# Stores of H and of the rows of x2 issued from ACT's queue instead of SyncE's

## The chip, the cores and the metric

The kernel runs on one core of a Trainium2 chip. The metric is the device time of one execution in microseconds (us). Five engines work side by side, each through its own list of instructions in a fixed order: TensorE (PE, with its weight loads as PEld), VectorE (DVE), ScalarE (ACT), GpSimd (POOL) and SyncE (SP), which computes nothing and issues transfers (DMAs). ACT and POOL can issue transfers too. An instruction that has to wait for a semaphore holds up what stands behind it on its own engine.

## The reference, cut to what matters

```python
scores = (q @ k.T) / sqrt(64); keep = (pos < 4) | ((0 <= rel) & (rel < 128))
x  = softmax(where(keep, scores, -1e9)) @ v       # 4 batches, 8 heads, 768 tokens -> 3072 x 512
H  = max(x @ w1, x @ w2, x @ w3)                  # 3072 x 768
x2 = H @ w_out                                    # 3072 x 512
# routing: tokens go to 8 experts by their logits x2 @ w_gate, 384 tokens to each expert
out[mask_e] = relu(x2[mask_e] @ u1[e]) @ u2[e]
```

## The kernel before, in words

The 3072 tokens are worked on as 8 groups of 384. Numbers are split into a high and a low part (h and l), and a product takes three matmuls: high by high, low by high and high by low.

- **Attention** (class Attn) works on one pair of heads at a time. SP loads kn, qn, vn and vns for it; these tiles have one buffer each. ACT and DVE split them (kh, kz, qs, vsp), PE makes scores, ACT and DVE make the softmax in a tile T, and PE transposes it and multiplies by v.
- **The first mixture** (Moe1.group) makes H for a group: for each of six blocks f, three times 12 matmuls into a PSUM tile mm (two buffers), taken over by ACT (i=0, L274) or DVE (i=1 and 2, L275) into hm (two buffers); ACT then makes hh (L279) and DVE hl (L280). Group 0 stores each hm to DRAM (sp), since w_out isn't there yet; group 5 stores all its hh and hl (sp0h, sp0l to sp5h, sp5l). Both are L282.
- **x2** (Moe1.x2) makes three row tiles of 128 tokens for a group: twice 18 matmuls (L296) into mm, which ACT copies (L298) into the two halves of xo. ACT copies the gate logits out of xo into LG (L306), and L307 stores the 512 columns of xo to x2d in DRAM. The tile xo has one buffer: the next row tile's first L298 can't write until the store before it has landed. This form of x2 runs five times: group 1, then group 0 (its H loaded back from sp by `reload`, L312), then groups 2, 3 and 4. That makes 15 stores. The last three groups use other tiles (xq, three buffers), and their stores were on ACT's queue already.
- **Routing and the second mixture** (Route, Moe2) follow from about 606 us on. They read x2d by indirect loads, and stream the experts' weights through SP.

All of the first part stands in one block whose order, on each engine, is set by a scheduler from priorities and modelled times: code marked `high_priority` is moved forward, attention of group g+1 is spread between the blocks of group g. So a DMA that is moved to another queue can move other instructions too. Each DMA waits on semaphores that the order's rows name: `DMAHW1` is the count of transfers that land on it, and `Activation` or `DVE` a count of instructions that these engines finished.

Of the kernel before, what the change touches and what calls it, by code (L numbers as in the profile page):

```python
# [22 lines left out]
def f32(ap): return ap.bitcast(FT)  # L23
# [179 lines left out]
class Moe1:  # L203
# [49 lines left out]
    def group(s,xs,spill=None,pair=False,pool=None,mid=None,between=None):  # L253

        nc=s.nc; main=s.main
        X=[]
        for p in range(4):
            h=main.tile([128,384],FR,name=f"xh{p}",bufs=1); l=main.tile([128,384],FR,name=f"xl{p}",bufs=1)
            with s.tc.high_priority():
                nc.scalar.activation(h,xs[p],AF.Copy)  # L260
                nc.vector.tensor_tensor(l,xs[p],f32(h),op=OP.subtract)  # L261
            X.append((h,l))
        H=[]
        for f in range(6):
            if between is not None: between(f)
            m=main.tile([128,384],FT,name="hm",bufs=2)
            for i in range(3):
                ps=s.mm.tile([128,512],FT,name="mm")
                n=0
                for p in range(4):  # L270
                    for a,b in ((0,0),(0,1),(1,0)):
                        nc.tensor.matmul(ps[:,:384],s.W[i][a][:,p,f*128:(f+1)*128],X[p][b],start=(n==0),stop=(n==11)); n+=1  # L272
                with s.tc.high_priority():
                    if i==0: nc.scalar.activation(m,ps[:,:384],AF.Copy)  # L274
                    else: nc.vector.tensor_tensor(m,ps[:,:384],m,op=OP.max)  # L275
                if mid is not None and (f,i)==s.at: mid()
            h,l=((pool or main).tile([128,384],FR,name=f"h{x}{f}",bufs=1) for x in "hl")
            with s.tc.high_priority():
                nc.scalar.activation(h,m,AF.Copy)  # L279
                nc.vector.tensor_tensor(l,m,f32(h),op=OP.subtract)  # L280
            if spill is not None:
                for d,x in (zip(spill[f],(h,l)) if pair else ((spill[f],m),)): nc.sync.dma_start(d,f32(x))  # L282
            H.append((h,l))
        return H
    def x2(s,H,t0,LG,x2d,n=260,pool=None,keep=None):

        nc=s.nc; main=s.main
        for t in range(3):
            o=pool.tile([128,512],FT,name="xq",bufs=3) if pool else main.tile([128,520],FT,name="xo",bufs=1)
            for u in range(2):  # L290
                c=slice(0,260) if n==260 else slice(4-4*u,260-4*u)
                ps=s.mm.tile([128,512],FT,name="mm")
                k=0
                for f in range(6):
                    for a,b in ((0,0),(0,1),(1,0)):
                        nc.tensor.matmul(ps[:,:n],H[f][a][:,t*128:(t+1)*128],s.WO[b][:,f,u,c],start=(k==0),stop=(k==17)); k+=1  # L296
                with s.tc.high_priority():
                    nc.scalar.activation(o[:,u*n:(u+1)*n],ps[:,0:n],AF.Copy)  # L298
                    if keep is not None:
                        for d in (2*u,2*u+1):  # L300
                            h,l=keep(t,d); c=ps[:,(d-2*u)*128:(d-2*u)*128+128]
                            nc.scalar.activation(h,c,AF.Copy)
                            nc.vector.tensor_tensor(l,c,f32(h),op=OP.subtract)
            if n==260:
                o,e=s.row(o,0)
                nc.scalar.activation(LG[:,t0+t,:].rearrange("p (u e) -> p u e",u=2),e,AF.Copy)  # L306
            (nc.scalar if pool else nc.sync).dma_start(x2d[(t0+t)*128:(t0+t+1)*128,:],o)  # L307
    def reload(s,spill):
        nc=s.nc; H=[]
        for f in range(6):  # L310
            m=s.main.tile([128,384],FT,name="hm",bufs=2)
            nc.sync.dma_start(m,spill[f])  # L312
            h=s.main.tile([128,384],FR,name=f"hh{f}",bufs=1); l=s.main.tile([128,384],FR,name=f"hl{f}",bufs=1)
            nc.scalar.activation(h,m,AF.Copy)  # L314
            nc.vector.tensor_tensor(l,m,f32(h),op=OP.subtract)
            H.append((h,l))
        return H
# [455 lines left out]
```

## Time and profile before

| | us |
|---|---|
| median of 3 runs (1009.89 to 1012.05) | 1010.73 |
| the profiled execution | 1006.23 |
| its span in the trace | 1004.5 |
| PE busy in the span | 943.2 |
| DVE busy | 715.4 |
| ACT busy | 534.6 |
| POOL busy | 344.9 |

The span runs from the first instruction to the last. An engine's busy time is the time in which at least one of its computing instructions ran; issuing a DMA doesn't count as busy, but it does occupy the engine's place in its own order. PE's busy time is modelled at the end of each matmul, so small gaps hide in it. [...]

### The profile page before, as it was taken

How to read it: one execution, taken by the hardware profiler on the slowest of the kernel's cores; microseconds unless marked ns; L12 is line 12 of the kernel's file. 1: busy time of each engine (PE TensorE's matmuls, PEld its weight loads, DVE VectorE, ACT ScalarE, POOL GpSimd, SP SyncE). 2: the span in 40 equal slices, each digit the busy share in tenths (PEclk: the TensorE clock that was granted, in tenths of full speed). 3: DMA queues.
4: the chain of work that ended last, by engine and by line, in shares of the span. 5: the costliest groups of instructions: out<-in, count | busy, mean ns of one | idle time of the engine just before them, and what ended most of it. 6: DMA issues, size and time to landing. Idle time of an engine off the chain costs nothing.

```text
span 1004.5 us, 18503 instructions
## 1 busy us (share of the span) xinstructions
PE 943.2 (94%) x6594; PEld 860.1 (86%) x6594; DVE 715.4 (71%) x1740; ACT 534.6 (53%) x1431; POOL 344.9 (34%) x307
## 2 busy tenths in 40 slices
PE   4879899989999999999999999989899999999996
PEld 3558799979999989999999998878788788888895
DVE  7989887785977898787754435887888888843320
ACT  5667664896868787688643211323434333454431
POOL 4677555045344535345533000101202111233331
PEclk9999899989999999999999999998999999999999
DMA  7444412231112112112210002623525443553430
GB/s 214 149 140 138 133 62 65 65 99 60 53 37 79 42 44 77 36 46 79 79 44 2 1 1 85 213 87 106 167 65 169 126 146 118 168 189 114 149 105 32
DMA packets 50541, 95.04 MB, mean 95 GB/s; under 512 B 6704, under 2 KB 20784, under 8 KB 50448
## 3 DMA queue, kind: packets, MB, share of 16 engines
q1 hardware_dynamic: 45312, 79.04, 25.4%
q0 software_dynamic: 3840, 12.45, 3.6%
q10 hardware_dynamic: 1296, 2.36, 0.6%
q8 instruction: 52, 0.85, 0.4%
q14 instruction: 41, 0.34, 0.1%
HBM read 77.84 MB, written 16.12 MB: 94 GB/s over the span
## 4 chain that ended last, share of the span: by engine, by line
PE 70%; DVE 11%; DMA 6%; ACT 5%; issue 5%; POOL 1%; SPq 0%; POOLq 0%; DVEq 0%; ACTq 0%
PE mm L272 27%; PE acc L594 11%; PE mm L601 11%; PE mm L296 5%; PE po L181 3%; DMA sa<-in_u_dram 3%; PE rc L399 2%; DMA st<-in_words_dram 2%; PE pp L25 2%; DVE qs L97 2%; PE pt L25 1%; PE po L172 1%; PE ps L126 1%; DVE cA L223 1%; PE ps L127 1%
## 5 line engine op out<-in xcount | busy, mean ns | idle before, releaser
L177 POOL TENSOR_TENSOR L<-A_w,H 128x768 fp32r<-128x768 f32 x46 | 87.4, 1900 | 141.0 <-ACT H L176 133.7
L556 POOL DMA_INDIRECT xg<-x2d,idx x24 | 26.1, 1088 | 192.0 <-PE mm L601 70.3
L275 DVE TENSOR_TENSOR hm<-mm,hm 128x384 f32<-128x384 f32 x96 | 53.2, 554 | 53.8 <-PE mm L272 51.9
L544 ACT ACTIVATE wah<-sa 128x512 fp32r<-128x512 f32 x64 | 40.5, 632 | 94.1 <-PE mm L601 65.4
L544 ACT ACTIVATE wbh<-sb 128x512 fp32r<-128x512 f32 x64 | 40.3, 630 | 73.7 <-PE acc L594 63.1
L594 PE MATMUL acc<-wbh,hh 128*128 128x512 f32 x192 | 78.3, 408 | 0.0
L594 PE MATMUL acc<-wbh,hl 128*128 128x512 f32 x192 | 78.2, 407 | 0.0
L594 PE MATMUL acc<-wbl,hh 128*128 128x512 f32 x192 | 77.7, 405 | 0.0
L296 PE MATMUL mm<-woh,hh 128*128 128x260 f32 (+1 forms) x252 | 73.7, 294 | 1.8 <-ACT hh L314 1.7
L296 PE MATMUL mm<-woh,hl 128*128 128x260 f32 (+1 forms) x252 | 72.2, 292 | 1.6 <-DVE hl L280 1.1
L296 PE MATMUL mm<-wol,hh 128*128 128x260 f32 (+1 forms) x252 | 72.2, 288 | 0.0
L272 PE MATMUL mm<-xh,w1h 128*128 128x384 f32 x192 | 66.8, 348 | 1.6 <-DVE hm L275 0.8
L545 DVE TENSOR_TENSOR wbl<-sb,wbh 128x512 fp32r<-128x512 f32 x64 | 44.1, 689 | 33.8 <-ACT wbh L544 33.7
L272 PE MATMUL mm<-xh,w0h 128*128 128x384 f32 x192 | 67.1, 349 | 0.5 <-DVE hm L275 0.5
L272 PE MATMUL mm<-xh,w2h 128*128 128x384 f32 x192 | 66.6, 347 | 0.8 <-ACT wgt L249 0.4
L272 PE MATMUL mm<-xl,w0h 128*128 128x384 f32 x192 | 65.3, 340 | 1.3 <-DVE xl L261 1.3
L272 PE MATMUL mm<-xh,w1l 128*128 128x384 f32 x192 | 65.7, 342 | 0.0
L272 PE MATMUL mm<-xl,w1h 128*128 128x384 f32 x192 | 65.6, 342 | 0.0
L272 PE MATMUL mm<-xl,w2h 128*128 128x384 f32 x192 | 65.0, 339 | 0.0
L272 PE MATMUL mm<-xh,w0l 128*128 128x384 f32 x192 | 65.0, 338 | 0.0
L272 PE MATMUL mm<-xh,w2l 128*128 128x384 f32 x192 | 64.9, 338 | 0.0
L605 DVE SCALAR_TENSOR_TENSOR hl<-mm,hh 128x384 fp32r<-128x384 f32 x64 | 35.3, 553 | 41.3 <-ACT hh L604 41.0
(315 smaller groups left out, 3090.7 us busy)
## 6 DMA issues: line engine op xcount, KB each, us to landing
sa<-in_u_dram SPq DMA_DIRECT2D x64, 256.0 KB
sb<-in_u_dram SPq DMA_DIRECT2D x64, 256.0 KB
st<-in_words_dram SPq DMA_DIRECT2D x24, 512.0 KB
qn<-in_q_dram SPq DMA_DIRECT2D x24, 192.0 KB
x2d<-xo SPq DMA_DIRECT2D x15, 256.0 KB
kn<-in_k_dram SPq DMA_DIRECT2D x12, 264.0 KB
vn<-in_v_dram SPq DMA_DIRECT2D x12, 256.0 KB
kn<-in_k_dram SPq DMA_DIRECT2D x12, 198.0 KB
```

The source lines that it names most:

```text
L25: nc.tensor.transpose(out,x,f32(ident))
L177: nc.gpsimd.tensor_tensor(L,Af,f32(H),op=OP.subtract)
L181: nc.tensor.matmul(po[:,q:q+n],u['VS'][:,blk,128*h:128*h+128],part[:,c:c+n],start=(part is H and j==0),stop=False,skip_group_check=True)
L272: nc.tensor.matmul(ps[:,:384],s.W[i][a][:,p,f*128:(f+1)*128],X[p][b],start=(n==0),stop=(n==11)); n+=1
L275: else: nc.vector.tensor_tensor(m,ps[:,:384],m,op=OP.max)
L296: nc.tensor.matmul(ps[:,:n],H[f][a][:,t*128:(t+1)*128],s.WO[b][:,f,u,c],start=(k==0),stop=(k==17)); k+=1
L544: nc.scalar.activation(h,src,AF.Copy)
L545: (nc.gpsimd if s.n>=6 and nm=="wa" else nc.vector).tensor_tensor(l,src,f32(h),op=OP.subtract)
L556: nc.gpsimd.indirect_dma_start(out=g,out_offset=None,in_=s.x2d[0:first or 3072],in_offset=bass.IndirectOffsetOnAxis(ap=idx[:,t:t+1],axis=0 ...
L594: nc.tensor.matmul(acc[t],H[f][a][:,t*128:(t+1)*128],W[f][1][b],start=(f==0 and n==0),stop=(f==F-1 and n==2)); n+=1
L601: nc.tensor.matmul(ps[:,:384],W[f][0][a][:,k,:],X[k][b],start=(n==0),stop=(n==11)); n+=1
L605: nc.vector.scalar_tensor_tensor(l,ps[:,:384],0.0,f32(h),op0=OP.max,op1=OP.subtract)
```

## The change

The stores of L282 and L307 are issued by ACT instead of SP. Nothing else in the source differs.

```diff
             if spill is not None:
-                for d,x in (zip(spill[f],(h,l)) if pair else ((spill[f],m),)): nc.sync.dma_start(d,f32(x))
+                for d,x in (zip(spill[f],(h,l)) if pair else ((spill[f],m),)): nc.scalar.dma_start(d,f32(x))
...
             if n==260:
                 o,e=s.row(o,0)
                 nc.scalar.activation(LG[:,t0+t,:].rearrange("p (u e) -> p u e",u=2),e,AF.Copy)
-            (nc.scalar if pool else nc.sync).dma_start(x2d[(t0+t)*128:(t0+t+1)*128,:],o)
+            nc.scalar.dma_start(x2d[(t0+t)*128:(t0+t+1)*128,:],o)
```

33 stores change queue: 6 of sp (group 0), 12 of sp0h to sp5l (group 5) and 15 of x2d. On PE the order is the same for the first 913 rows (up to the end of x2 of groups 1 and 0); behind that attention and first mixture are interleaved otherwise, up to group 6, and the rest is the same again.

ACT, first row tile of x2 in group 1. Before, from the copy of the logits (L306) on to the next row tile's L298:

```order
L96 ACTIVATE qs_2866<-qn 64x384
L306 ACTIVATE LG<-xo 128x8 [waits Activation_49]
L145 ACTIVATE l<-l 128x6 [waits Activation_49]
L134 ACTIVATE T_w<-ps 128x132 [waits PE_49,Pool_49]
L298 ACTIVATE xo<-mm 128x260 [waits DMAHW1_49,Activation_49]
L298 ACTIVATE xo<-mm 128x260
```

The same place in the changed kernel:

```order
L96 ACTIVATE qs_2866<-qn 64x384
L306 ACTIVATE LG<-xo 128x8 [waits Activation_49]
L307 DMA x2d<-xo 128x512 [waits DMAHW1_49]
L145 ACTIVATE l<-l 128x6 [waits Activation_49]
L134 ACTIVATE T_w<-ps 128x132 [waits PE_49,Pool_49]
L298 ACTIVATE xo<-mm 128x260 [waits DMAHW1_49,Activation_49]
L298 ACTIVATE xo<-mm 128x260
```

The store now stands behind L306 on ACT, two short instructions ahead of the L298 that waits for it to land.

SP at the same x2, as a difference (kn and qn are loads of attention, hm the reload of group 0's H):

```order
 L77 DMA qn<-in_q_dram 128x384
 L312 DMA hm<-sp_1038 128x384
-L307 DMA x2d<-xo 128x512
-L75 DMA kn<-in_k_dram 128x528
-L307 DMA x2d<-xo 128x512
+L75 DMA kn<-in_k_dram 128x528
 L77 DMA qn<-in_q_dram 128x384
 L312 DMA hm<-sp_1039 128x384
-L307 DMA x2d<-xo 128x512
 L312 DMA hm<-sp_1040 128x384
```

The loads keep their order and lose the three stores between them; before, the stores did not stand behind L306 but followed the second L298.

ACT, the first block of group 5, whose hh and hl are stored. Before:

```order
L279 ACTIVATE hh_5382<-hm 128x384 [waits DVE_49]
L274 ACTIVATE hm<-mm 128x384 [waits PE_49]
L108 ACTIVATE vsp<-vn 128x4x2x64 [waits DMAHW4_49,PE_49]
L183 ACTIVATE x_5679<-po 64x384 [waits PE_49]
L142 ACTIVATE m<-m 128x6 [waits DVE_49]
```

And in the changed kernel:

```order
L279 ACTIVATE hh_5382<-hm 128x384 [waits DVE_49]
L282 DMA sp0h<-hh_5382 128x384 [waits DMAHW6_49,Activation_49]
L282 DMA sp0l<-hl_5383 128x384 [waits DVE_49]
L274 ACTIVATE hm<-mm 128x384 [waits PE_49]
L183 ACTIVATE x_5679<-po 64x384 [waits PE_49]
```

The two stores stand between hh and the next takeover from PSUM (L274), and the second one waits on ACT for DVE's hl.

## Rows read from the trace of the kernel before

**Rows 1.** The page: span, and busy time of each engine.

```profile
span 1004.5 us, 18503 instructions
PE 943.2 (94%) x6594; PEld 860.1 (86%) x6594; DVE 715.4 (71%) x1740; ACT 534.6 (53%) x1431; POOL 344.9 (34%) x307
```

**Rows 2.** Stretches: us, busy (count) of PE, PEld, DVE, ACT, POOL; PEclk, DMA share, GB/s.

```profile
77.00:195.00 118.00, 112.52 (x693) 105.55 (x691) 96.89 (x175) 76.41 (x210) 61.13 (x54) 0.97 0.29 91
195.00:210.00 15.00, 13.78 (x109) 13.09 (x110) 11.14 (x22) 14.77 (x55) 5.58 (x3) 1.00 0.32 97
210.00:230.00 20.00, 14.79 (x86) 12.88 (x84) 18.41 (x32) 18.45 (x55) 8.70 (x6) 0.82 0.30 88
230.00:242.00 12.00, 12.00 (x91) 11.99 (x90) 7.38 (x11) 7.70 (x27) 8.25 (x7) 0.87 0.30 102
242.00:530.00 288.00, 283.18 (x1906) 277.49 (x1905) 221.04 (x398) 211.50 (x615) 133.04 (x115) 1.00 0.18 55
```

**Rows 3.** Chain that ended last, 186 to 245 us: start, us, what.

```profile
206.12 1.16 ACT T_w L144 x5
...
219.43 4.21 DMA hm<-sp
...
229.45 0.66 PE po L181 x3
```

**Rows 4.** SP's waits, whole run: us in total, times, longest.

```profile
SPq L307 <- ACT xo L298: 26.1, 6, 9.0
...
SPq L282 <- ACT hh L279: 18.8, 4, 9.0
```

**Rows 5.** All engines' waits for a transfer, 77 to 606 us.

```profile
ACT st L221 <- DMA st<-in_words_dram: 1.9, 2, 1.7
...
ACT xo L298 <- DMA x2d<-xo: 1.4, 1, 1.4
```

**Rows 6.** Timeline of SP, 180 to 245 us: start, length, what.

```profile
197.83 0.33 SPq L307 DMA_DIRECT2D x2d<-xo  x1
...
204.13 0.32 SPq L307 DMA_DIRECT2D x2d<-xo  x1
```

**Rows 7.** Timeline of ACT, 190 to 240 us.

```profile
203.08 0.21 ACT L306 ACTIVATE LG<-xo 128x8 f32<-128x8 f32 x1
...
203.45 0.65 ACT L298 ACTIVATE xo<-mm 128x260 f32<-128x260 f32 x2
...
205.49 0.19 ACT L306 ACTIVATE LG<-xo 128x8 f32<-128x8 f32 x1
...
207.70 0.36 ACT L298 ACTIVATE xo<-mm 128x260 f32<-128x260 f32 x1
```

**Rows 8.** Timeline of SP, 447 to 467 us.

```profile
450.45 0.43 SPq L307 DMA_DIRECT2D x2d<-xo  x1
```

**Rows 9.** Timeline of ACT, 448 to 463 us: in brackets idle time before, and who ended it.

```profile
454.64 0.39 ACT L298 ACTIVATE xo<-mm 128x260 f32<-128x260 f32 x1 [1.44 <-DMA x2d<-xo]
```

**Rows 10.** Stretches around the first store of x2, columns as in Rows 2.

```profile
198.50:199.70 1.20, 1.20 (x12) 1.20 (x11) 0.90 (x2) 1.15 (x3) 0.00 (x0) 1.00 0.60 219
```

**Rows 11.** Timeline of ACT, 614 to 665 us: a store from ACT and its neighbour.

```profile
641.44 0.36 ACTq L331 DMA_DIRECT2D x2d<-xq  x1
641.85 1.09 ACT L330 ACTIVATE xq<-acc 128x512 f32<-128x512 f32 x2 [0.44 <-PE acc L327]
```

**Rows 12.** Chain that ended last, 640 to 650 us.

```profile
641.44 4.56 DMA x2d<-xq
```

**Rows 13.** Chain that ended last, 300 to 316 us: x2 of group 2.

```profile
304.74 4.30 PE mm L296 x36
...
309.78 4.30 PE mm L296 x36
```

**Rows 14.** Timeline of SP, 245 to 520 us: the first two stores of group 5.

```profile
474.93 0.33 SPq L282 DMA_DIRECT2D sp0h<-hh  x1
...
478.68 0.33 SPq L282 DMA_DIRECT2D sp0l<-hl  x1
```

## Prediction

> **What bounds the kernel now.** I read the page first: TensorE is busy for 943.2 of 1004.5 us, ACT for 534.6 [rows 1]. Then I cut the span where the changed stores lie [rows 2]. From 242 to 530 us PE is busy for 283.18 of 288.00 us, so that stretch is PE's: only 4.82 us are to be won there, and ACT (211.50) has 76.5 us to spare. Between 195 and 230 us it is otherwise: ACT is busy for 14.77 of 15.00 us and then 18.45 of 20.00, while PE idles for 1.22 and 5.21 us. The chain of work says the same: it runs over ACT's softmax and the reload of H and is back on PE at 229.45 us [rows 3]. This is where x2 of group 1 runs, with three of the 33 stores. From 77 to 195 us PE idles for 5.48 us with ACT at 76.41 of 118 [rows 2].
>
> Next, what the stores do on SP today. SP sat for 26.1 us behind L307 and 18.8 us behind L282 [rows 4], and loads stood behind them. But hardly anybody waited for a load: from 77 to 606 us the largest waits for a transfer are 1.9 us (two weight loads) and 1.4 us (xo for its own store) [rows 5]. SP's waiting is slack.
>
> **What the change removes.** 33 issues of about 0.33 us [rows 6] leave SP, 10.9 us, off the path, since no engine waited for the loads behind them. One wait could shrink: a store issued at 450.45 us held back ACT's L298 for 1.44 us [rows 8, 9]. I count a gain of 0.5 us, between 0 and the sum of rows 5, 3.3.
>
> **What it adds: the wait for xo.** xo has one buffer, so the next row tile's L298 waits until the store has landed. SP issued the store directly behind the second L298 (at 197.83 us [rows 6]), while ACT was at other work until 203.08. On ACT it stands behind L306, as the order's rows show, and only two short instructions ahead of that next L298, which started at 203.45 us [rows 7]. So the transfer, which before ran beside 5 us of ACT's work, now lies in front of ACT.
>
> How long does a store take to land? The trace doesn't give it directly, so I bound it. Its data moved in the 1.20 us up to 199.70 us (219 GB/s over 1.20 us are its 256 KB [rows 10]), so it cannot have landed earlier than about 1.9 us after its issue. The store of 450.45 us let L298 go at 454.64 [rows 8, 9], 4.2 us; the slowest one on the chain took 4.56 us [rows 12]. The second store here, issued at 204.13 us, had landed by 207.70 [rows 6, 7], so in at most 3.6. I take 3.0 us, between 1.9 and 4.56.
>
> First store: issued at about 203.3 us (behind L306), landed at 206.3, where L298 started at 203.45: 2.8 us. ACT may take the issue a little ahead of its arithmetic; I count 2.5. Second store: its L306 moves from 205.49 to 208.0 us, so it is issued at 208.2 and lands at 211.2, where L298 would be due at 207.70 + 2.5 = 210.2: 1.0 more. ACT is thus 3.5 us late by 211 us. It carries on through a chain of ACT, DVE and reload with about 1.55 us of free ACT time [rows 2]; I take 1.0 off, and PE gets its next work **2.5 us** later. With 1.9 us to land, 1.4 us of wait is left, which the free time swallows: 0. With 4.56, the first wait is 4.4 and the second 2.5: 6.9 us. Lost PE time isn't won back later, since what follows is PE's stretch.
>
> Second x2 (group 0, 230 to 242 us): PE is busy without a gap and ACT only for 7.70 of 12 us [rows 2]. 0.3 us, 0 to 1.
>
> The other three sets (groups 2 to 4, nine stores): the same wait stands on ACT, but PE has two mm buffers. In group 2, PE begins its second row tile at 304.74 and its third at 309.78 us [rows 13]; an L298 that is 2 us late frees its buffer just in time for the third. ACT has about a quarter of its time free. 1.0 us together, 0 to 4.
>
> **The issues themselves.** ACT issuing a store takes 0.36 us, and its next activation began 0.05 us behind it [rows 11]: 0.4 us each, 13 us over the 33, if all of it is in ACT's way. For the 15 stores of x2 it is in the sums above or in ACT's free quarter. For the 18 of L282 it is 7 us, where ACT has 41.6 us free (77 to 195) and a quarter of its time (to 530) [rows 2]. The low halves cost more: sp0l left SP 3.75 us after sp0h [rows 14], for want of DVE's hl, and on ACT such a wait stands in front of L274, which frees a PSUM buffer. Cover is the second mm buffer, about 2 us. 0.5 us, 0 to 2.
>
> **The order behind 242 us** changes on PE, ACT and DVE. There PE has 4.82 us idle now [rows 2], so a better order gains at most that; I take 0, from -2 to +2.
>
> **Sum.** 2.5 + 0.3 + 1.0 + 0.5 - 0.5 + 0 = 3.8 us on a span of 1004.5, or 1006.2 to 1010.0 us for the profiled execution. The runs' median, 1010.73, is 4.5 us above that execution; I put the difference onto the median: 1014.5 us.
>
> **The rivals.** What a measurement of this kernel can tell from no change is about 0.2%, 2.0 us.
>
> - *No change.* Stores land in about 2 us, the free ACT time between 210 and 230 us takes up the wait, and the mm buffers cover the rest: 0 + 0 + 0.3 + 0.3 = 0.6 us, about 1011. For it speaks that PE, not ACT, binds in most of the block. Against it, that at 195 to 210 us ACT has 0.23 us free. [...]
> - *ACT becomes the bound at every x2.* Landing near 4.5 us, first set 6.9 us, groups 2 to 4 another 4: with 0.5 for the low halves about 11 us, 1022. It decides if L298 is late by more than the 4.30 us of a row tile's matmuls [rows 13].
> - *Faster.* SP's loads no longer sit behind stores (26.1 and 18.8 us [rows 4]), attention's inputs come earlier, and the new order closes most of the 4.82 us that PE idles between 242 and 530 us, while the wait for xo costs less than 1: about -3 us, 1007.7. It decides when PE's idle in that stretch falls under 2 us. For it: the loads do come earlier. Against it: no engine waits for one [rows 5]. [...]
>
> **How the numbers follow.** Forecast (+2 to +7 us) 0.46, no change 0.27, ACT as the bound 0.14, faster 0.13. The predicted time is the forecast's, 1014.5; its own range is 1012.7 to 1017.7. The range for 8 in 10 leaves out most of the faster case and the far end of the ACT case: 1009 to 1021. Slower by over 0.2%: 0.46 and 0.14, 0.60; within 0.2%: 0.27; faster: 0.13.
>
> **What the changed profile would show.** L298 of xo on ACT waiting for x2d<-xo at the second and third row tile of group 1, 2 to 3 us and about 1 us; PE's idle from 195 to 230 us up from 6.4 to about 9; PE's idle from about 245 to 535 us still near 5; no load waited for, before or after. The prediction is wrong if L298 hardly waits (landing is faster, or the issue runs well ahead of ACT's arithmetic), if that wait is there and PE doesn't feel it, or if the new order behind 242 us moves PE's idle by more than the whole sum.

## The result and the profile after

The changed kernel takes 1015.66 us (median of 8 runs, 1012.74 to 1018.61), the kernel before 1010.75 (8 runs, 1009.32 to 1012.09). The ratio is 1.0051, 95% interval 1.0034 to 1.0068: 4.9 us slower. I had predicted 1014.5 us, slower. The number is nearly right, but the runs below show that most of its steps are not: waits of ACT were to cost 4.3 us, less a gain of 0.5, and they cost next to nothing; the loss comes from a term that I had put at 0.

The page of the changed kernel, in answer to [rows 1]:

```profile
span 1015.4 us, 18487 instructions
...
PE 947.5 (93%) x6594; PEld 862.7 (85%) x6594; DVE 713.6 (70%) x1740; ACT 536.0 (53%) x1431; POOL 345.0 (34%) x307
```

Its stretches, in answer to [rows 2], with the same columns (PEclk is TensorE's granted clock as a share of full speed):

```profile
77.00:195.00 118.00, 113.47 (x704) 106.34 (x702) 98.01 (x177) 77.02 (x213) 62.50 (x53) 0.99 0.30 93
195.00:210.00 15.00, 14.36 (x106) 13.95 (x105) 10.04 (x20) 13.97 (x49) 5.21 (x3) 0.89 0.26 81
210.00:230.00 20.00, 14.82 (x90) 13.23 (x88) 18.56 (x33) 18.68 (x58) 8.54 (x6) 0.83 0.29 88
...
242.00:530.00 288.00, 279.56 (x1863) 272.31 (x1862) 214.76 (x392) 208.69 (x608) 128.41 (x111) 0.99 0.18 54
```

From 195 to 230 us, where I expected PE's idle time to rise from 6.4 to about 9 us, it is 0.64 + 5.18 = 5.8 us. From 242 to 530 us, where I expected it to stay near 5, it is 8.44 us against 4.82.

The step that I rested most on is seen in ACT's timeline at x2 of group 1, in answer to [rows 6, 7]:

```profile
199.83 0.33 ACTq L307 DMA_DIRECT2D x2d<-xo  x1
...
201.87 0.21 ACT L306 ACTIVATE LG<-xo 128x8 f32<-128x8 f32 x1
...
203.14 0.66 ACT L298 ACTIVATE xo<-mm 128x260 f32<-128x260 f32 x2
...
204.02 0.33 ACTq L307 DMA_DIRECT2D x2d<-xo  x1
...
207.34 0.36 ACT L298 ACTIVATE xo<-mm 128x260 f32<-128x260 f32 x1
```

The store stands behind L306 in the program, but ACT's sequencer (ACTq) issued it at 199.83 us, 2.0 us before L306 ran. It had landed before L298 wanted xo at 203.14 us, and no idle time stands before that L298. I had put the issue at 203.3 us.

**Where the time went.** PE's order is that of before up to its 1220th matmul and again from its 3114th, with the same matmuls between. On DVE and ACT a few instructions change places from about 80 us on, but PE's 1220th matmul starts no later for it (239.88 against 242.01 us). So this work can be compared from the start of the same matmul to the start of the same matmul. At five places inside, too, both orders have done equally many matmuls of every line; the pieces between these are compared likewise. The kernel before (columns as in [rows 2]; the first row is the whole of it):

```profile
242.01:528.11 286.10, 281.28 (x1896) 275.59 (x1894) 219.52 (x396) 210.03 (x613) 131.33 (x113) 1.00 0.18 55
...
300.52:320.93 20.41, 19.45 (x149) 18.86 (x148) 15.60 (x33) 17.85 (x50) 9.08 (x8) 1.00 0.26 82
...
326.52:361.11 34.59, 34.59 (x223) 34.22 (x222) 29.46 (x45) 24.13 (x65) 18.20 (x16) 1.00 0.17 51
361.11:442.24 81.13, 78.31 (x533) 76.80 (x532) 66.49 (x124) 61.64 (x187) 36.54 (x31) 1.00 0.16 49
442.24:528.11 85.87, 84.83 (x572) 81.97 (x571) 59.70 (x106) 59.97 (x181) 39.72 (x32) 1.00 0.20 64
```

The changed kernel:

```profile
239.88:532.77 292.89, 284.45 (x1895) 276.88 (x1894) 218.79 (x397) 210.23 (x612) 129.68 (x112) 0.99 0.18 54
...
298.40:321.35 22.95, 21.05 (x149) 20.49 (x149) 19.53 (x33) 19.65 (x58) 11.01 (x8) 0.93 0.23 69
...
326.94:364.57 37.63, 35.30 (x223) 34.19 (x222) 29.70 (x53) 27.69 (x77) 20.12 (x17) 1.00 0.17 47
364.57:443.80 79.23, 77.43 (x533) 76.23 (x531) 61.14 (x116) 58.10 (x168) 34.14 (x30) 1.00 0.17 50
443.80:532.77 88.97, 86.56 (x572) 82.31 (x571) 62.67 (x111) 62.01 (x189) 38.43 (x31) 1.00 0.19 62
```

The same matmuls take 6.8 us longer: 2.5, 3.0 and 3.1 us more in three pieces and 1.9 less in one (the rest of the stretch is equal). What PE waits for in the first two is in its waits (us in total, times, longest), 298 to 365 us:

```profile
PE mm L272 <- DVE hm L275: 2.3, 3, 1.1
PE ps L126 <- DVE T_w L131: 1.0, 1, 1.0
PE ps L126 <- DVE T_w L135: 0.6, 1, 0.6
```

None of these is a store or a load. DVE's timeline shows why hm (L275) was late:

```profile
333.32 2.08 DVE L95 TENSOR_TENSOR kz<-kn,kh_w 64x528 fp32r<-64x528 f32 x1
...
336.92 0.56 DVE L275 TENSOR_TENSOR hm<-mm,hm 128x384 f32<-128x384 f32 x1
...
342.11 2.22 DVE L97 TENSOR_TENSOR qs<-qn,qs 64x384 fp32r<-64x384 f32 x1
344.37 0.56 DVE L275 TENSOR_TENSOR hm<-mm,hm 128x384 f32<-128x384 f32 x1
```

L275 hands a PSUM buffer back to PE, and here it stands behind a kz and a qs that take 2.08 and 2.22 us; another qs of that size took 0.55 us at 336.34. The kernel before has a slow kz here too (2.60 us at 329.92), but its L275 stands in front of it, and PE waits for nothing in this piece. The long qs runs while POOL's L177 does:

```profile
342.06 1.86 POOL L177 TENSOR_TENSOR L<-A_w,H 128x768 fp32r<-128x768 f32 x1 [7.23 <-ACT H L176]
```

POOL's L177 ends at 343.92 us and the qs 0.41 us later. Over the changed kernel's whole run, all 24 kz and qs that take over 1 us run at least partly beside an instruction of POOL; of the 72 shorter ones 17 do. Why they are longer there is not shown.

My theory after this trace: the loss is the new order of this stretch, not the queue. The rival: ACT's waits on its own queue (2.7 us for x2d<-xo, and for DVE's hl in front of L274) slow the chain in place, whatever the order.

### The profile page after: what moved, and what is told of

The parts are those of the page before. It is cut to its first block, busy times and chain, and to the rows that moved or that the text cites. A ratio compares the mean times of both kernels' runs of the same rounds, so it can differ in the third digit from the quotient of the medians.

```text
span 1015.4 us, 18487 instructions
## 1 busy us (share of the span) xinstructions
PE 947.5 (93%) x6594; PEld 862.7 (85%) x6594; DVE 713.6 (70%) x1740; ACT 536.0 (53%) x1431; POOL 345.0 (34%) x307
## 4 chain that ended last, share of the span: by engine, by line
PE 67%; DVE 12%; ACT 7%; issue 7%; DMA 4%; POOL 2%; SPq 0%; POOLq 0%; ACTq 0%; DVEq 0%
PE mm L272 23%; PE mm L601 11%; PE acc L594 11%; PE mm L296 5%; PE po L181 3%; PE rc L399 2%; DMA st<-in_words_dram 2%; PE pt L25 2%; DVE qs L97 2%; PE pp L25 1%; DVE cA L223 1%; DMA sa<-in_u_dram 1%; PE acc L327 1%; ACT T_w L144 1%; PE po L172 1%
## 5 line engine op out<-in xcount | busy, mean ns | idle before, releaser
L177 POOL TENSOR_TENSOR L<-A_w,H 128x768 fp32r<-128x768 f32 x46 | 87.7, 1906 | 108.2 <-ACT H L176 108.2
L275 DVE TENSOR_TENSOR hm<-mm,hm 128x384 f32<-128x384 f32 x96 | 53.1, 553 | 49.0 <-PE mm L272 45.6
L272 PE MATMUL mm<-xh,w2h 128*128 128x384 f32 x192 | 66.9, 348 | 0.8 <-ACT hm L274 0.4
```

The source lines that it names most:

```text
L177: nc.gpsimd.tensor_tensor(L,Af,f32(H),op=OP.subtract)
```

## The experiments

Each ratio is against the kernel before on the same chip, with its 95% interval. The chips differ (before takes 1011.3, 1002.5 and 1002.3 us in the three groups of runs), so ratios and stretches are compared, not times. A single profiled span says little: those of before and of e1 differ by 8.5 us (1004.5 and 1013.0), with their stretches of 242 to 528 us only 1.2 us apart and the same order behind it.

**e1 to e4: queue or order.** To part the two, the instructions of each engine are chained in a given order. The chain is meant to set the order alone (its links are of the class NoSync): e1, chained in before's order, takes 0.9999 of before's time.

```diff
-        with tc.block(schedule_with_timeline_sim=True):
+        with tc.block(schedule_with_timeline_sim=True),pinned(tc):
...
+@contextmanager
+def pinned(tc):
...
+    yield
...
+    by={i.name:i for i in tc.nc.cur_bb.bb.instructions}; prev=0
+    info=bass.mybir.DependencyInfo(bass.mybir.DependencyClass.NoSync,bass.mybir.DependencyReason.DATA)
+    for n in od:
...
+        if n and prev: tc.add_manual_dep(by[f"I-{n}"],f"I-{prev}",info,reason="pin")
+        prev=n
```

Here od is a list of instruction numbers, engine by engine. e1 takes the changed kernel with before's list (each store put behind its L306 or L279), e2 the kernel before with the changed kernel's.

e1, the queue alone.

> All 33 stores on ACT's queue, but on every engine the order of the kernel before is kept (the stores alone are put in behind L306 and behind L279 on ACT; SP's loads keep their order). Theory 'order' (the loss comes from the new order behind 242 us): no change, -2 to +1 us, PE's idle from 242 to 530 us near 5 us. Rival 'in place' (ACT waits for DVE's hl and for its own stores, whatever the order): +4 to +6 us, PE's idle in that stretch up to 9 us or more. The prediction's own sum without the order term: +3.8 us, with L298 of group 1 waiting 2 to 3 us.

Measured: 0.9999 (0.9976 to 1.0022), 1011.66 us against 1011.3. Its stretch of the same matmuls:

```profile
240.94:528.27 287.33, 282.60 (x1894) 276.55 (x1894) 217.83 (x396) 211.47 (x614) 132.77 (x113) 0.99 0.18 55
```

PE idles for 4.73 us in it. Yet ACT did wait for hl:

```profile
ACT hm L274 <- DVE hl L280: 2.7, 1, 2.7
ACT T_w L134 <- DVE hl L280: 2.5, 2, 1.5
...
ACT x L183 <- DVE hl L280: 1.2, 1, 1.2
```

PE's longest wait for ACT in that stretch is 0.3 us. So moving all 33 stores costs nothing measurable, although ACT waits 6.4 us for hl. The rival, which wanted 4 us or more, falls; a loss of up to 2.2 us, the end of the interval, isn't excluded.

e2, the order alone.

> All 33 stores stay on SP, but every engine runs in the order of the changed kernel (SP's loads too; a store stands on SP behind the same load as before). Theory 'order': +3 to +6 us, about as slow as the changed kernel, PE's idle from 242 to 535 us up by about 6 us. Rival 'in place': 0, -1 to +1 us. If both this and the run with the queue alone show half of it, both causes share the loss.

Measured: 1.0039 (1.0020 to 1.0058), with every store on SP.

```profile
238.72:530.43 291.71, 283.47 (x1895) 276.86 (x1894) 215.54 (x397) 210.96 (x612) 129.35 (x112) 0.99 0.17 54
```

8.24 us of idle time, as in the changed kernel (8.44). With no store moved, the order alone brings most or all of the loss (0.39% here, 0.51% in the changed kernel; the intervals overlap).

e3, three stores with PE's order unchanged:

```diff
-            (nc.scalar if pool else nc.sync).dma_start(x2d[(t0+t)*128:(t0+t+1)*128,:],o)
+            (nc.scalar if pool or t0==3 else nc.sync).dma_start(x2d[(t0+t)*128:(t0+t+1)*128,:],o)
```

> Only the three x2 stores of group 1 are issued from ACT; the order of PE, DVE and POOL is that of before. The prediction's term for this set: +2.5 us, between 0 and 6.9, with L298 waiting for its store. Theory 'ACT issues ahead of its arithmetic' (as the changed kernel's trace shows, store at 199.83 us with L298 starting at 203.14 us without a wait): 0, between -1 and +0.5 us, and PE no later at 242 us than before.

Measured: 0.9996 (0.9972 to 1.0020); 2.5 us would be 1.0025, just outside. ACT again issued ahead, and L298 followed without a wait:

```profile
200.27 0.35 ACTq L307 DMA_DIRECT2D x2d<-xo  x1
...
203.61 0.66 ACT L298 ACTIVATE xo<-mm 128x260 f32<-128x260 f32 x2
```

e4, the same edit with t0==0, in group 0.

> Only the three x2 stores of group 0 (230 to 242 us) are issued from ACT; 30 stores stay on SP, but the build gives PE, DVE, ACT and POOL nearly the order of the changed kernel from 242 us on. Theory 'order': +3 to +6 us, as much as all 33 stores. Rival 'in place': a loss in proportion to the stores, 3 of 33, at most +0.5 us.

Measured: 1.0038 (1.0019 to 1.0058). Three stores cost about as much as 33, because they make the build choose nearly the whole new order:

```profile
238.95:531.14 292.19, 283.92 (x1895) 277.04 (x1894) 217.24 (x397) 210.47 (x612) 129.30 (x112) 0.99 0.17 54
```

Over these six profiles, the stretch takes 286.1, 287.3 and 289.1 us in before's order (before, e1, e3) and 292.9, 291.7 and 292.2 in the new one (after, e2, e4), means of 287.5 and 292.3. The 4.8 us between them agree with the 4.9 of the result. PE's idle time is 4.7 to 4.9 us in the first three, 8.2 to 8.4 in the others, 3.5 us of the 4.8; the other 1.3 are in PE's busy time, and what they are is not shown. Outside the stretch, the same six executions take between 716 and 726 us, whatever the order, so the profiles alone would not show the loss; the ratios do.

The clock is not the difference. In the new order it falls at about 302 us (0.93 over 298 to 321 us in the changed kernel). But in before's order it falls too in two of the three profiles: its share is 0.93 over 360.00 to 384.15 us in e1, and 0.87 over 359.75 to 385.38 us in e3. And over all executions on this chip the mean granted clock is 0.980 in before and in e1, 0.979 in e3, 0.981 in e2 and 0.982 in e4.

**e5 to e7: which part of the order.** The list is put together from the two orders, cut at about 329 and 448 us, where all engines have issued the same instructions in both. All 33 stores are on ACT. In words:

```diff
-od = order of before
+od = order of the changed kernel up to 329 us, before's from there    (e5)
+od = order of the changed kernel from 329 to 448 us, before's else    (e6)
+od = order of before up to 448 us, the changed kernel's from there    (e7)
```

e5.

> All 33 stores on ACT; the changed kernel's order up to about 329 us, then that of before. Theory 'places' (the new order loses at definite places, here at 298 to 321 us, where PE waits for T_w): PE needs 22.9 us for the work that takes it 20.4 us in before's order, PE's idle there 1.9 instead of 0.96 us with a granted clock of 0.93, in all +2.5 us. Rival 'whole' (the loss hangs on the order as a whole and is not to be put at a place): this piece alone costs 0, and the 20.4 us stay.

Measured: 1.0049 (1.0030 to 1.0068). Its trace has the idle time of the changed kernel at 298 to 302 us, but not what follows it there. The changed kernel:

```profile
298.40:302.20 3.80, 1.90 (x12) 1.38 (x11) 3.63 (x12) 3.73 (x14) 0.09 (x1) 0.98 0.03 6
302.20:305.40 3.20, 3.20 (x16) 3.20 (x17) 3.05 (x4) 3.10 (x8) 3.20 (x2) 0.50 0.21 84
```

And e5:

```profile
298.31:302.20 3.89, 2.00 (x13) 1.48 (x13) 3.61 (x12) 3.82 (x14) 0.20 (x1) 1.00 0.01 2
302.20:305.40 3.20, 3.20 (x28) 3.20 (x28) 3.15 (x4) 3.10 (x8) 3.20 (x2) 1.00 0.21 84
```

Here the granted clock was 0.50 for 3.2 us, after 1.9 us of idle time, and PE made 16 matmuls instead of 28; there it stayed at 1.00. So the profiled execution of e5 loses 1.0 us in this piece, not 2.5. It was also the fastest of e5's seven (1000.8 us, their median 1006.27). What the others lost is not shown; it was not the clock, whose mean over all executions is 0.981 in e5 and in before.

e6.

> All 33 stores on ACT; the changed kernel's order from about 329 to 448 us alone, before's elsewhere. Theory 'places': 37.6 us instead of 34.6 for the work of 326 to 361 us (PE waits for DVE's hm), and about 1 to 3 us given back from 361 to 448 us: in all 0 to +2 us. Rival 'whole': 34.6 us there, no loss.

Measured: 0.9995 (0.9983 to 1.0007). Two rows of it:

```profile
323.82:358.75 34.93, 34.62 (x224) 34.09 (x223) 28.42 (x49) 26.52 (x74) 19.50 (x17) 1.00 0.17 50
...
437.82:526.72 88.90, 85.94 (x573) 81.81 (x571) 60.44 (x110) 62.66 (x191) 39.62 (x33) 1.00 0.19 62
```

The first goes against "places": the piece with the late hm takes 34.9 us in the changed order as well, if before's order ran ahead of it. The second is before's own order and takes 3.0 us longer than in before. By these two rows, a piece's price hangs on how the engines come into it.

e7.

> All 33 stores on ACT; before's order up to about 448 us, then the changed kernel's. Theory 'places': 87.7 to 89.0 us instead of 85.9 to 86.4 for the work of 442 to 528 us, PE's idle there above 2 us instead of 1.04: in all +1.3 to +3 us. Rival 'whole': 86 us.

Measured: 1.0059 (1.0037 to 1.0080), more than either expectation; 69.2 and 22.8 us in its two halves (before and changed kernel: 66.9 and 69.6, then 18.9 and 19.4). The second row is a stall that neither parent has:

```profile
508.65:531.45 22.80, 20.68 (x120) 17.53 (x120) 12.92 (x22) 11.94 (x35) 7.21 (x6) 1.00 0.13 48
```

The three parts alone come to +4.9, -0.5 and +5.9 us, 10 together, where the whole order costs 4.9. They don't add up, so "places" is right only in that the whole new order loses at the same places each time (the piece of 37.63 us takes 37.74 in e2 and 37.69 in e4).

**e8: one of these places.** In the changed kernel, two L275 on DVE are moved ahead; nothing else is:

```diff
+L275 TENSOR_TENSOR hm<-mm,hm 128x384
 L95 TENSOR_TENSOR kz_111<-kn,kh_w 64x528
 L154 TENSOR_TENSOR psb_109<-pt,psb_109 8x384
 L135 COPY_PREDICATED T_x<-ca,ps 128x128
 L97 TENSOR_TENSOR qs_4687<-qn,qs_4687 64x384
-L275 TENSOR_TENSOR hm<-mm,hm 128x384
...
+L275 TENSOR_TENSOR hm<-mm,hm 128x384
 L97 TENSOR_TENSOR qs_4688<-qn,qs_4688 64x384
-L275 TENSOR_TENSOR hm<-mm,hm 128x384
```

> The changed kernel, with two instructions moved on DVE: two takeovers L275 (hm), which in the changed kernel's trace start at 336.92 and 344.37 us, go ahead of the kz (2.08 us) and the qs (2.22 us) that they stand behind. If PE loses its time from 326.9 to 364.6 us because these stand behind slow DVE work: 35.5 to 36 us there instead of 37.6, and about +3 us against before in place of +4.9. Rival (DVE as a whole is late there, and what is put behind is waited for next): still 37.6 us.

Measured: 1.0022 (1.0007 to 1.0037), where the changed kernel had 1.0051. The piece that took 37.63 us:

```profile
327.65:362.72 35.07, 34.80 (x224) 34.16 (x223) 27.80 (x53) 27.61 (x77) 20.10 (x17) 1.00 0.19 50
```

2.33 us of idle time became 0.27. So in the changed kernel this loss came from where two instructions stood on DVE. DVE's work in this piece got shorter with the move (29.70 us busy before it, 27.80 with it, 53 instructions each), so how much is due to L275 no longer standing behind slow work, and how much to that work being shorter, is not parted. The ratios of the two kernels come from different chips, and their intervals overlap a little.

**e9, e10: what the queue can cost.** In e6 the prediction's term for L282 does show. PE:

```profile
475.86 0.44 PE L272 MATMUL mm<-xh,w2h 128*128 128x384 f32 x1 [1.42 <-ACT hm L274]
```

and ACT:

```profile
471.53 0.33 ACTq L282 DMA_DIRECT2D sp0h<-hh  x1
474.95 0.33 ACTq L282 DMA_DIRECT2D sp0l<-hl  x1
475.32 0.49 ACT L274 ACTIVATE hm<-mm 128x384 f32<-128x384 f32 x1 [3.82 <-DVE hl L280]
```

The low half's store holds ACT for DVE's hl, with L274 behind it, 3.82 us, of which PE feels 1.42. e9 puts each such store behind the next L274:

```diff
 L282 DMA sp0h<-hh_5382 128x384
+L274 ACTIVATE hm<-mm 128x384
 L282 DMA sp0l<-hl_5383 128x384
-L274 ACTIVATE hm<-mm 128x384
```

> The kernel of e6 (all 33 stores on ACT, changed order from 329 to 448 us alone), with the six stores of low halves (hl, groups 5) put behind the next L274 on ACT instead of in front of it. In e6, PE waited 1.42 us for that L274 at 474 us, which stood behind such a store. If the prediction's term for L282 (0.5 us, 0 to 2) is this wait: it is gone, PE needs 68 us instead of 69.4 for the work of 442 to 509 us, and the time falls by 1.4 us, to about 0.998 of before. If L274 then only waits for something else: 69.4 us stay.

Measured: 0.9985 (0.9967 to 1.0002), against 0.9995 for e6, which is not to be told apart. The wait for L274 is gone, but L108 now stands behind the store:

```profile
ACT vsp L108 <- DVE hl L280: 3.0, 1, 3.0
```

and PE waits 1.17 us at 479.47 for DVE's x instead. Its stretch of 442 to 509 us takes 70.8 us, not 68 and not 69.4. Neither expectation held as it stood: L274 no longer waits for the store, but the wait moved on to others.

e10 has e6's order with the 33 stores back on SP (as e2 has the changed kernel's).

> The order of e6 on every engine, but all 33 stores on SP, as before. Theory 'order' (the queue itself costs nothing but such waits): as e9, about 0.998 of before, PE's wait for L274 at 474 us gone. Rival (ACT's queue costs or gains by itself): over 2 us away from e9.

Measured: 0.9988 (0.9971 to 1.0004). With the same order but for the stores, ACT's queue and SP's give the same time within 0.2%. No run here beats before by more than can be told.

**e11, e12: another order, with no store moved.** The number that raises the priority of attention's instructions is changed:

```diff
-off=60
+off=58   (e11)
+off=61   (e12)
```

e11.

> All stores on SP, as before; the one number that sets the priority of attention's instructions is 58 instead of 60, which gives another order of about the same distance from before as the changed kernel's (1709 lines of difference on PE, against 1628). Theory 'order' (any new order of this stretch may cost or gain some us): between -3 and +8 us, with PE's idle from 242 to 530 us other than 5 us. Rival 'before's order is nothing special': within 1 us of before.

Measured: 1.0121 (1.0099 to 1.0143). PE from 242 to 540 us in e11 (in before it is busy there for 293.18 us):

```profile
242.00:540.00 298.00, 286.25 (x1888) 281.33 (x1886) 211.06 (x396) 211.10 (x612) 131.80 (x115) 0.97 0.17 53
```

e12.

> As the run with 58, with 61 (2657 lines of difference on PE, from earlier in the span). Theory 'order': between -3 and +8 us. Rival: within 1 us of before.

Measured: 1.0058 (1.0036 to 1.0080), with PE busy for 290.02 of those 298 us. With no store moved, three other orders (these and e2) lose 4 to 12 us, e11 by more than I had allowed; a fourth, e10's, neither loses nor gains. In e11 the clock is lower too: its mean is 0.974 over all executions, against 0.981 in before.

## Why the prediction was right in its number and wrong in its reasons

- **What bounds the kernel, and the stores' place on SP.** Right: 242 to 530 us is PE's stretch, and taking 33 issues off SP won nothing that can be measured (e1).
- **The wait for xo (2.5 us, group 1).** Wrong: 0. I let ACT's sequencer issue the store when its arithmetic reached it. It issued 2.0 us before L306 ran, and the store landed under other work of ACT, as before. Five activations, from the L94 that starts at 199.82 us to L306, were still to end when the store was issued at 199.83. The time to land varies more than I allowed (1.9 to 4.56 us): in the changed kernel the stores issued at 199.83 and 204.02 us kept no L298 waiting at 203.14 and 207.34, so they landed in at most 3.3 us; one issued at 453.11 us let L298 go at 457.99, after 4.9 us.
- **Second x2 and groups 2 to 4 (0.3 and 1.0 us).** L298 did wait in the later sets, 2.7 us in two waits. With before's order it was 0.3 us in all, and PE lost nothing (e1).
- **The issues and the low halves (0.5 us, 0 to 2).** The mechanism is there: 1.42 us in e6, in one place. In e1 PE did not feel it, and once moved it left its time to the next wait (e9).
- **The order behind 242 us (0, from -2 to +2).** This is the step that failed: it is +4.8 us between the means, +3.9 us in e2's ratio (0.0039 of 1011). I had seen that there were only 4.82 us to win and took nought as the middle; there was far more to lose. Its bound of +2 had no row behind it.
- **The sum** hit by luck: 3.8 us of waits that did not come stand for 4.8 us of order that I had left out. I had named signs of being wrong. One came: L298 hardly waits, since the issue runs ahead of ACT's arithmetic. Another, that the new order moves PE's idle by more than the whole sum, was narrowly missed: 3.6 us in the profiles of before and after, against 3.8.
- **The rivals.** "No change" describes the queue alone: 0.9999 in e1. Between e9 (0.9985, stores on ACT) and e10 (0.9988, on SP) the queue makes no difference that can be told. "Faster" would have needed a better order; the builds tried gave worse ones, or in e6, e9 and e10 ones that can't be told from before's.

Open: why the piece of 326 to 361 us is slow only behind the changed order (e6), what e5's other runs lost, what the 1.3 us of PE's busy time are, and whether an order exists that wins more than 0.2%.

## What to carry to other kernels

Where a scheduler sets the order by modelled times, an edit of one instruction's queue is two changes: the queue, and a new order of everything behind it. Part them by pinning the order before giving either the credit, and compare the stretch between the same two matmuls, since whole spans of equal orders lie up to 8.5 us apart. Even such stretches lie 3.0 us apart (before and e3, where the clock fell), so the credit goes by many runs. In a stretch that the bounding engine fills to 98%, an unforeseen new order has more room to lose than to win; its term in a sum is not nought.

## What was not expected of the hardware

ACT's sequencer issued a DMA 2.0 us ahead of the activation in front of it in the program, in the changed kernel and in e3 alike. And equal idle time of PE, 1.9 us at the same place, was followed by 3.2 us at a granted clock of 0.50 in one kernel's execution and by none in another's (rows of e5 above). One and the same order shows both: with 1.9 us of idle time between about 360 and 385 us, the clock stayed at 1.00 in before and fell in e1 and e3.
